# Norms in vector steps instead of a GpSimd power, a first triangle loaded in quarters, and a planner that looks ahead, in a delta-rule and two-MLP kernel

## The chip, the cores and the metric

The kernel runs on one core of one Trainium2 chip. The metric is device time in microseconds (us) of one execution. The profile is of one execution; its engines are PE (TensorE), DVE (VectorE), ACT (ScalarE), POOL (GpSimd) and SP (SyncE, which here only issues DMAs).

## The reference, cut to what matters

```python
# attention: batch 4, heads 8, 768 steps, head size 48
k_n = k / (np.linalg.norm(k, axis=-1, keepdims=True) + 1e-06)
for t in range(S):
    y[:, :, t] = np.einsum('bhd,bhde->bhe', q[:, :, t], state)
    v_old = np.einsum('bhde,bhd->bhe', state, kt)
    state = state + bt[:, :, :, None] * np.einsum('bhd,bhe->bhde', kt, vt - v_old)
# first MLP on 3072 tokens, 384 -> 1024 -> 384
h = x @ w_in
e = np.exp(h - np.max(h, axis=-1, keepdims=True))
solu = h * (e / (np.sum(e, axis=-1, keepdims=True) + 1e-09))
ln = (solu - mu) / np.sqrt(var + 1e-06) * g_ln        # mu, var over the 1024
x = ln @ w_out
# second MLP, 384 -> 2048 -> 384
h = x @ w_in2
g = h * (1.0 / (1.0 + np.exp(-1.702 * h)))
out = g @ w_out2
```

## The kernel before, in words

The 768 steps are cut into 24 chunks of 32 (`CH`). For a chunk, the recurrence inside it is a triangular system. `gram(n)` multiplies keys with keys and queries on PE, DVE masks the result (L659) and SP stores it to DRAM (`g_dr`, L681). Four chunks make one macro chunk (`m`, 0 to 5). `solve(m)` loads the four key products as one tile `tri` of 128 x 32 x 32 (L753; L706 in `solve0`), so that every partition holds one triangle. `roots` takes the diagonal, which holds the squared norms of the keys, raises it to the power 0.5 on POOL (L689) and makes from it, in five small DVE instructions (L694 to L698), the norm, its inverse square times beta, and the negative of that. The triangle is scaled and inverted by elimination on DVE (L768, L771; L722, L724 in `solve0`, which inverts two half triangles), scaled once more (`dsb`) and sent through DRAM to be laid out by chunk (`dt`). `recur(n)` (`first_recur` for the first four chunks) then carries the state through chunk n. `layer1(n)` is the first MLP up to its layer norm (tags A0 to A23), `layer1_out(g)` its second product for a group of four chunks (B0 to B5, L1122), `layer2(g)` the second MLP (C0 to C5, L1157 and L1184).

The weights come as 8-byte floats. `weights` loads a block into a stage buffer (L542), rebuilds single precision with ACT and DVE (L545, L549, L554, L562), and splits it into two half-precision parts (L575; L581, L582 on PE and L584 on ACT). This work stands beside the first four chunks. The setup also prepares two products for the first four chunks from the PSUM bank of the gram: `edges` on ACT (L670) and `place` on DVE (L674).

All five engines run their instructions in order, in an order that a planner writes at build time. Each piece of work is a task with an engine, a guessed duration, a priority and the keys that it reads and writes. The planner (`emit`) holds a clock for each engine; of the tasks of an engine that could start first it takes the one of lowest priority number. Priorities are a due time plus an offset from a table (`OFF`, one number for each tag and engine). Tasks of the first macro chunk have priorities below -20000 (up to -100000), and their tags get the letter F; before, the table held offsets of about the same size for those tags, which bring these priorities back to near zero, among those of the weights. Parameters stand in `PRM`. `busy` lets the planner fill an idle PE with products of zeros (L422).

Of the kernel before, what the change touches and what calls it, by code (L numbers as in the profile page):

```python
# [16 lines left out]
CH = 32  # L17
# [103 lines left out]
class Plan:  # L121
# [47 lines left out]
    def emit(self, sem=SEM, log=None):  # L169
        for t in self.tasks:  # L170
            t.left = len(t.deps)
            for d in t.deps:
                d.outs.append(t)
        for t in reversed(self.tasks):
            t.work2 = t.dur + (t.lat + LAND if t.lat else 0.0) + max([o.work2 + (sem if o.eng != t.eng or t.lat else 0.1) for o in t.outs], default=0.0)
        top = max(t.work2 for t in self.tasks)
        if PRM["al"]:
            for t in self.tasks:
                t.prio = (1 - PRM["al"]) * t.prio + PRM["al"] * PRM["af"] * (top - t.work2)
        free = {}  # L180
        pend = {}
        dma_free = 0.0
        bank_free = [0.0] * 8
        held = [False] * 8

        def place(b):
            open_ = [(bank_free[i], k, i) for k, i in enumerate(b.where) if not held[i]]
            return min(open_) if open_ else None

        for t in self.tasks:  # L190
            free.setdefault(t.eng, 0.0)
            pend.setdefault(t.eng, [])
            if t.left == 0:
                pend[t.eng].append(t)
        done = 0
        small, near = False, 0.0
        port = {"DVE": 0.0, "POOL": 0.0}
        clock = Clock()
        fetch = Fetch(clock)
        n = len(self.tasks)  # L200
        while done < n:
            cand = None
            for e, ts in pend.items():
                if not ts:
                    continue
                e0 = free[e]
                opts = []
                for t in ts:
                    st = max(e0, t.ready)
                    if t.lat:  # L210
                        st = max(st, dma_free - PRM["la"])
                    ok = True
                    for b in t.banks:
                        if b.at is None:
                            p = place(b)
                            if p is None:
                                ok = False
                                break
                            st = max(st, p[0])
                    if ok:  # L220
                        opts.append((st, t))
                if not opts:
                    continue
                first = min(o[0] for o in opts)
                opts = [o for o in opts if o[0] <= first + 1e-6]
                if e == "PE" and small:
                    opts = [o for o in opts if o[1].small and o[1].prio <= near] or opts
                st, t = min(opts, key=lambda o: (o[1].prio, o[1].idx))
                if cand is None or (st, t.prio, t.idx) < cand[0]:
                    cand = ((st, t.prio, t.idx), t)  # L230
            if cand is None:
                raise RuntimeError("no task can run")
            st, t = cand[0][0], cand[1]
            switch = t.eng == "PE" and t.small != small
            if t.eng == "PE":
                small, near = t.small, t.prio + PRM["near"]
            pend[t.eng].remove(t)
            for b in t.banks:
                if b.at is None:
                    b.at = place(b)[2]  # L240
                    held[b.at] = True
            dur = t.dur
            if t.eng == "PE":
                for gate, until, filler in self.fill:
                    if gate.end is None or held[0] or st > until:
                        continue
                    lo = max(free["PE"], gate.end + sem)
                    while True:
                        clock.run(lo, 0.0, 1.0)
                        if not (st - lo > (PRM["fg"] if clock.warm else 0.5) or clock.warm and clock.behind(lo) > 0.0):  # L250
                            break
                        filler()
                        free["PE"] = lo = fetch.run(lo, 0.216, 1.0, 2)
                st = max(st, free["PE"]) + (SWITCH[t.small] if switch else 0.0)
                dur = fetch.run(st, dur, t.work, t.count) - st
            elif t.port:
                other = port["POOL" if t.eng == "DVE" else "DVE"]
                dur = max(st + PORT[t.eng], other) + dur - PORT[t.eng] - st
                port[t.eng] = st + dur
            if log is not None:  # L260
                log.begin()
            t.fn()
            if log is not None:
                log.append((st, t))
            free[t.eng] = st + dur - TAIL.get(t.eng, 0.0)
            if t.lat:
                s2 = max(dma_free, st + dur)
                dma_free = s2 + t.lat
                t.end = s2 + t.lat + LAND
            else:  # L270
                t.end = st + dur + (DRAIN if t.eng == "PE" else 0.0)
            for b in t.banks:
                b.users -= 1
                if b.users == 0:
                    held[b.at] = False
                    bank_free[b.at] = t.end + sem
            for o in t.outs:
                o.left -= 1
                o.ready = max(o.ready, t.end + (sem if o.eng != t.eng or t.lat else OWN[t.eng] - (DRAIN if t.eng == "PE" else 0.0)))
                if o.left == 0:  # L280
                    pend[o.eng].append(o)
            done += 1
        return max(t.end for t in self.tasks)
# [3 lines left out]
def kernel(  # L287
# [160 lines left out]
    def dve(n, f=1.0):  # L448
        return 0.145 + f * n / 960.0
# [180 lines left out]
    def gram(n):  # L630
# [33 lines left out]
        if m == 0:  # L664
            v = bank_view = lambda: bank(bk).rearrange("p (h c) -> p h c", h=H)

            def edges():
                for b in range(B):
                    r, x = slice(32 * b, 32 * b + 16), 32 * (b % 2)
                    ACT.activation(out=EB[s][r, :, x + 16:x + 32], in_=v()[r, :, 16:32], func=ACTF.Copy)  # L670
            P.add("ACT", 1.2, edges, r=[bk], w=[f"E{s}"], prio=-3e4 + n)

            def place():
                DVE.tensor_tensor(  # L674
                    out=PB[s].rearrange("p h (x c) -> p h x c", x=2), in0=v()[:, :, CH:].unsqueeze(2).to_broadcast([128, H, 2, CH]),
                    in1=pm.unsqueeze(1).to_broadcast([128, H, 2, CH]), op=ALU.mult)
            P.add("DVE", dve(512), place, r=[bk, "pm"], w=[f"P{s}"], prio=-3e4 + n)
        else:
            P.add("DVE", dve(256), ev(p_, CH), r=[bk, "mask"], w=[gp[1]], prio=late)
# [7 lines left out]
    def roots(m, diag, prio):  # L687
        n_, c_, nn = nrm[:, 0], nrm[:, 1], nrm[:, 2]
        P.add("POOL", 0.8, lambda: POOL.tensor_tensor(  # L689
            out=nn, in0=diag, in1=half[:, 0:1].to_broadcast([128, CH]), op=ALU.pow),  # L690
            r=["tri", "half"], w=["nrm0", "nrm1"], prio=prio)

        def factors():
            DVE.tensor_scalar(out=n_, in0=nn, scalar1=1e-6, scalar2=None, op0=ALU.add)  # L694
            DVE.tensor_tensor(out=nn, in0=n_, in1=n_, op=ALU.mult)
            DVE.reciprocal(out=c_, in_=nn)
            DVE.tensor_tensor(out=c_, in0=c_, in1=btb[:, m], op=ALU.mult)
            DVE.tensor_scalar(out=nn, in0=c_, scalar1=-1.0, scalar2=None, op0=ALU.mult)  # L698
        P.add("DVE", 1.2, factors, r=["bt"], w=["nrm0", "nrm1"], prio=prio, port=True)

    def solve0():
        P.tag = "solve0"
        base = -9e4
        hc = CH // 2
        n_, c_, nn = nrm[:, 0], nrm[:, 1], nrm[:, 2]
        P.add("SP", ISSUE, lambda: SP.dma_start(out=tri, in_=g_dr[0]),  # L706
              r=[f"gdr0_{s}" for s in range(SUB)], w=["tri"], prio=base - 5, lat=dma(524288))
        roots(0, tri.rearrange("p i j -> p (i j)")[:, 0:CH * CH:CH + 1], base)
        cut = lambda x: x.rearrange("p (a i) -> p a i", a=2).unsqueeze(3).to_broadcast([128, 2, hc, hc])
        small = blocks[:, :, 0:hc, 0:hc]  # L710

        def scale():
# [555 lines left out]
```

## Time and profile before

| | |
|---|---|
| median of 3 runs | 848.41 us (845.32 to 852.46) |
| profiled execution | 848.33 us |
| its span, first to last instruction | 846.6 us |
| PE busy | 772.3 us (91%) |
| DVE busy | 550.9 us (65%) |
| ACT busy | 394.8 us (47%) |
| POOL busy | 285.9 us (34%) |
| mean granted TensorE clock | 0.968 |

The profiled execution took 848.33 us by the device's measure, 1.7 us more than its span. Busy shares are averages over a start of about 150 us, in which the first four chunks and the weights are worked on, and a long rest, in which PE works through the MLPs.

### The profile page before, as it was taken

Reading aid. Unit: us, or ns where it says so; the run is one execution under the profiler, and the core shown is the slowest. Engines: PE = TensorE matmul, PEld = TensorE weight load, DVE = VectorE, ACT = ScalarE, POOL = GpSimd, SP = SyncE. Lnnn points to the kernel's source line nnn. Section 1 sums busy time; section 2 is a strip of 40 time slices with the busy share of each in tenths; the row PEclk is TensorE's granted clock in tenths of the full one; section 3 lists DMA queues with packets and bytes.
Section 4 is the critical chain, followed back from the end, with each engine's and each line's share of the span. In section 5 each row is a group of like instructions: output and inputs, shape, how many; then the busy total and the mean of one; then the engine's idle time right before and its main releaser. Section 6 shows DMA issues by size and latency. Waiting matters only on the chain.

```text
span 846.6 us, 23757 instructions
## 1 busy us (share of the span) xinstructions
PE 772.3 (91%) x9981; PEld 390.7 (46%) x9981; DVE 550.9 (65%) x1324; ACT 394.8 (47%) x713; POOL 285.9 (34%) x259
## 2 busy tenths in 40 slices
PE   4399898979988999989998899999999999999997
PEld 3156664435544444444444344444444444444443
DVE  2677659968999898699965799765544283531111
ACT  4497548723655524435343444354445155452332
POOL 4230142032145713535331733522354024230322
PEclk9799899989999999989999999999999999999999
DMA  8788997844567836764457342544443342210000
GB/s 194 247 226 236 194 203 173 231 116 102 129 121 187 145 98 163 164 147 104 106 127 177 95 82 71 145 84 134 98 117 59 90 118 59 37 25 26 13 1 37
DMA packets 176922, 103.23 MB, mean 122 GB/s; under 512 B 127664, under 2 KB 163376, under 8 KB 176816
## 3 DMA queue, kind: packets, MB, share of 16 engines
q1 hardware_dynamic: 176816, 101.73, 51.0%
q8 instruction: 78, 1.28, 0.7%
q14 instruction: 28, 0.23, 0.1%
HBM read 64.26 MB, written 20.12 MB: 100 GB/s over the span
## 4 chain that ended last, share of the span: by engine, by line
PE 52%; DVE 30%; ACT 5%; DMA 4%; POOL 4%; issue 4%; SPq 1%; POOLq 0%; ACTq 0%; DVEq 0%
PE psum L1184 14%; PE psum L1157 13%; PE psum L1122 8%; PE psum L1050 7%; DVE trip L771 5%; DVE trt L768 4%; POOL nrm L689 3%; DVE mv L1011 3%; DVE thg L1165 2%; DVE eb L1069 2%; DVE mv L960 2%; DMA trip<-gdr 2%; PE psum L827 1%; PE psum L581 1%; DVE col L1057 1%
## 5 line engine op out<-in xcount | busy, mean ns | idle before, releaser
L1184 PE MATMUL psum<-thg,wo2h 128*128 128x512 f16 x576 | 192.3, 384 | 10.8 <-DVE thg L1174 5.0
L1171 POOL TENSOR_TENSOR thg<-thg 128x512 f16<-128x512 f32 x90 | 108.3, 1203 | 230.8 <-ACT thg L1168 152.4
L1157 PE MATMUL psum<-x2t,w2h 128*128 128x512 f16 x576 | 173.1, 382 | 2.0 <-DVE thg L1165 1.5
L1165 DVE SCALAR_TENSOR_TENSOR thg<-thg,psum 128x512 f32<-128x512 f32 x96 | 65.5, 683 | 87.6 <-ACT thg L1162 87.3
L1184 PE MATMUL psum<-thg,wo2l 128*128 128x512 f16 x288 | 110.6, 384 | 0.0
L1157 PE MATMUL psum<-x2t,w2l 128*128 128x512 f16 x288 | 110.1, 382 | 0.0
L1050 PE MATMUL psum<-w1h,xt 128*128 128x512 f16 x288 | 94.4, 391 | 5.0 <-DMA xt<-ysb 4.5
L1168 ACT ACTIVATE thg<-thg 128x512 f16<-128x512 f32 x96 | 60.2, 627 | 80.5 <-DVE thg L1165 78.8
L1162 ACT ACTIVATE thg<-psum 128x512 f32<-128x512 f32 x96 | 56.9, 593 | 81.1 <-PE psum L1157 80.5
L1184 PEld LDWEIGHTS <-wo2h 128*128 128x128 f16 x576 | 56.9, 99 | 77.6 <-issue 13.7
L1157 PEld LDWEIGHTS <-w2h 128*128 128x128 f16 x576 | 53.4, 98 | 64.7 <-issue 4.2
L771 DVE TENSOR_TENSOR trip<-trip,trt 128x30 f32<-128x30 f32 (+9 forms) x150 | 70.5, 470 | 2.8
L1066 ACT ACTIVATE eb<-psum,col 128x512 f32<-128x512 f32 x48 | 37.0, 773 | 75.2 <-DVE col L1062 70.6
L768 DVE TENSOR_TENSOR trt<-trip 128x30 f32<-128x30 f32 (+9 forms) x150 | 69.1, 460 | 2.5
L1050 PEld LDWEIGHTS <-xt 128*128 128x128 f16 x432 | 41.9, 100 | 58.1 <-issue 7.4
L1099 POOL TENSOR_TENSOR lnr<-eb,lnr 128x1024 f16<-128x1024 f32 x22 | 47.2, 2146 | 36.8 <-ACT lnr L1097 36.8
L1050 PE MATMUL psum<-w1l,xt 128*128 128x512 f16 x144 | 56.0, 389 | 0.0
L1122 PE MATMUL psum<-lnth,wo1h 128*128 128x512 f16 x144 | 54.6, 379 | 0.4 <-DVE eb L1069 0.4
L1122 PE MATMUL psum<-lnth,wo1l 128*128 128x512 f16 x144 | 54.6, 379 | 0.0
L1122 PE MATMUL psum<-lntl,wo1h 128*128 128x512 f16 x144 | 54.6, 379 | 0.0
L1057 DVE TENSOR_REDUCE col<-psum 128x1 f32<-128x512 f32 x48 | 32.9, 685 | 28.3 <-PE psum L1050 28.2
L1011 DVE SCALAR_TENSOR_TENSOR mv<-psum,mv 48x384 f32<-48x384 f32 x76 | 42.2, 555 | 12.4 <-PE psum L996 10.5
(208 smaller groups left out, 1178.3 us busy)
## 6 DMA issues: line engine op xcount, KB each, us to landing
kq<-kq SPq DMA_DIRECT2D x44, 192.0 KB, 4.6
stg<-w_in SPq DMA_DIRECT2D x13, 512.0 KB, 5.6
stg<-w_out SPq DMA_DIRECT2D x17, 384.0 KB, 4.2
vt<-vt SPq DMA_DIRECT2D x24, 192.0 KB, 3.3
kt<-kdr SPq DMA_DIRECT2D x48, 96.0 KB, 2.4
stg<-udr SPq DMA_DIRECT2D x48, 96.0 KB, 2.3
out<-ob SPq DMA_DIRECT2D x18, 256.0 KB, 2.1
st<-qt SPq DMA_DIRECT2D x40, 96.0 KB, 3.2
```

The source lines that it names most:

```text
L768: DVE.tensor_tensor(out=tv, in0=tri[:, lo:hi, j:j + 1].to_broadcast([128, nr, j]), in1=tri[:, j:j + 1, 0:j].to_broadcast([128, nr, j]), op ...
L771: DVE.tensor_tensor(out=tri[:, lo:hi, 0:j], in0=tri[:, lo:hi, 0:j], in1=tv, op=ALU.add)
L1011: P.add("DVE", dve(384), lambda sv=sv, r0=r0, e=e: DVE.scalar_tensor_tensor(out=sv, in0=bank(b4[e])[r0:r0 + D, 0:H * D], scalar=1.0 / (KS_ ...
L1050: PE.matmul(bank(bh[j]), lhsT=x[:, k], rhs=w_[:, k, 512 * j:512 * j + 512], start=(k == 0 and i == 0), stop=(k == K0 - 1 and i == 2))
L1099: P.add("POOL", pool(F1), lambda: POOL.tensor_tensor(out=ln_[1], in0=e_, in1=ln_[0], op=ALU.subtract), r=[lk[0]] + [f"eb{ie}_{j}" for j in ...
L1122: PE.matmul(bank(ba)[:, 0:w_], lhsT=wo1[a][:, k, oc], rhs=lnt[b][:, k, tk], start=(k == 0 and i == 0), stop=(k == K1 - 1 and i == 2))
L1157: PE.matmul(bank(bh)[:, 0:w_], lhsT=w2[a][:, k, fc], rhs=x2t[b][:, k, tk], start=(k == 0 and j == 0), stop=(k == K0 - 1 and j == 2))
L1162: P.add("ACT", act(w_), lambda: ACT.activation(out=th, in_=bank(bh)[:, 0:w_], func=ACTF.Tanh, scale=0.851 / (X2S * W2S)), r=[bh], w=[f"th{ ...
L1165: P.add("DVE", dve(w_), lambda: DVE.scalar_tensor_tensor(out=th, in0=th, scalar=1.0, in1=bank(bh)[:, 0:w_], op0=ALU.add, op1=ALU.mult), r= ...
L1168: P.add("ACT", act(w_), lambda: ACT.activation(out=gh, in_=th, func=ACTF.Copy), r=[f"th{i}"], w=[f"gh{i}"], prio=base)
L1171: P.add("POOL", pool(w_), lambda: POOL.tensor_tensor(out=gl, in0=th, in1=gh, op=ALU.subtract), r=[f"th{i}", f"gh{i}"], w=[f"gl{i}"], prio= ...
L1184: PE.matmul(bank(acc[o])[:, 0:w_], lhsT=wo2[a][:, f, oc], rhs=gb[i][b][:, 0:w_], start=(f == 0 and j == 0), stop=(f == K2 - 1 and j == 2))
```

## The change

Four edits. First, `roots` has no POOL instruction. DVE makes a first guess of a square root from the bits of the float (three instructions), then does three Newton steps of three instructions each (a reciprocal and two products), then the five instructions of `factors` as before. These are five tasks instead of a POOL task and a DVE task, in all six solves. Second, `solve0` loads its tile in four quarters of 32 partitions, each of which waits only for the store of its own chunk. Third, in the planner: on SP, DVE and ACT, a task of the first macro chunk (priority below -20000) that can start within 1.5, 0.3 or 0.3 us of the first possible start is taken ahead of everything else. `place` may not start before 15 us of the planner's clock. Fourth, the table of offsets: the 64 offsets of the F tags and of POOL in the solves are gone (so the first macro chunk keeps its priorities below -20000), and the other 485 all have new values. Three guessed durations in `solve0` are a little smaller.

```diff
+PRM = dict(kDVE=0.3, kACT=0.3, kPOOL=0.0, kPE=0.0, kSP=1.5, ...
                 first = min(o[0] for o in opts)
+                soon = [o for o in opts if o[1].prio < -2e4 and o[0] <= first + PRM["k" + e]] if PRM["k" + e] > 0 else []
+                if soon:
+                    st, t = min(soon, key=lambda o: (o[1].prio, o[1].idx))
+                    if cand is None or (st, t.prio, t.idx) < cand[0]:
+                        cand = ((st, t.prio, t.idx), t)
+                    continue
...
-            P.add("DVE", dve(512), place, r=[bk, "pm"], w=[f"P{s}"], prio=-3e4 + n)
+            P.add("DVE", dve(512), place, r=[bk, "pm"], w=[f"P{s}"], prio=-3e4 + n, nb=15.0)
...
     def roots(m, diag, prio):
         n_, c_, nn = nrm[:, 0], nrm[:, 1], nrm[:, 2]
-        P.add("POOL", 0.8, lambda: POOL.tensor_tensor(
-            out=nn, in0=diag, in1=half[:, 0:1].to_broadcast([128, CH]), op=ALU.pow),
-            r=["tri", "half"], w=["nrm0", "nrm1"], prio=prio)
+        u_, t_, s2 = nrm[:, 3], nrm[:, 2], nrm[:, 1]
+
+        def guess():
+            ui = u_.bitcast(I32)
+            DVE.tensor_scalar(out=s2, in0=diag, scalar1=2.0, scalar2=None, op0=ALU.mult)
+            DVE.tensor_scalar(out=ui, in0=diag.bitcast(I32), scalar1=1, scalar2=None, op0=ALU.logical_shift_right)
+            DVE.tensor_scalar(out=ui, in0=ui, scalar1=0x203D1DF5, scalar2=None, op0=ALU.add)
+
+        def heron():
+            DVE.reciprocal(out=t_, in_=u_)
+            DVE.tensor_tensor(out=t_, in0=s2, in1=t_, op=ALU.mult)
+            DVE.scalar_tensor_tensor(out=u_, in0=u_, scalar=0.5, in1=t_, op0=ALU.mult, op1=ALU.add)
 
         def factors():
-            DVE.tensor_scalar(out=n_, in0=nn, scalar1=1e-6, scalar2=None, op0=ALU.add)
+            DVE.tensor_scalar(out=n_, in0=u_, scalar1=0.5, scalar2=1e-6, op0=ALU.mult, op1=ALU.add)
...
-        P.add("DVE", 1.2, factors, r=["bt"], w=["nrm0", "nrm1"], prio=prio, port=True)
+        for f, d in ((guess, 0.55), (heron, 0.8), (heron, 0.8), (heron, 0.8), (factors, 1.2)):
+            P.add("DVE", d, f, r=["tri", "bt"], w=["nrm0", "nrm1"], prio=prio, port=True)
 
     def solve0():
...
-        P.add("SP", ISSUE, lambda: SP.dma_start(out=tri, in_=g_dr[0]),
-              r=[f"gdr0_{s}" for s in range(SUB)], w=["tri"], prio=base - 5, lat=dma(524288))
+        for s in range(SUB):
+            rows = slice(32 * s, 32 * s + 32)
+            P.add("SP", ISSUE, lambda rows=rows: SP.dma_start(out=tri[rows], in_=g_dr[0][rows]),
+                  r=[f"gdr0_{s}"], w=["tri"], prio=base - 5, lat=dma(131072))
...
-        P.add("DVE", 8.2, halves, w=["tri"], prio=base, port=True)
+        P.add("DVE", 7.8, halves, w=["tri"], prio=base, port=True)
...
-        P.add("DVE", 1.5, lambda: DVE.tensor_tensor(
+        P.add("DVE", 1.0, lambda: DVE.tensor_tensor(
```

## Rows read from the trace of the kernel before

**Rows 1.** The page, parts 1 and 4: busy times, and the chain by line

```profile
PE 772.3 (91%) x9981; PEld 390.7 (46%) x9981; DVE 550.9 (65%) x1324; ACT 394.8 (47%) x713; POOL 285.9 (34%) x259
PE psum L1184 14%; PE psum L1157 13%; PE psum L1122 8%; PE psum L1050 7%; DVE trip L771 5%; DVE trt L768 4%; POOL nrm L689 3%; DVE mv L1011 3%; DVE thg L1165 2%; DVE eb L1069 2%; DVE mv L960 2%; DMA trip<-gdr 2%; PE psum L827 1%; PE psum L581 1%; DVE col L1057 1%
```

**Rows 2.** Windows by stage: busy time of each engine, granted clock, DMA share, GB/s

```profile
0.00:41.00 41.00, 15.63 (x330) 9.64 (x331) 18.49 (x56) 17.44 (x39) 15.10 (x39) 0.88 0.86 227
...
71.00:154.00 83.00, 75.90 (x1529) 47.72 (x1528) 59.38 (x167) 52.13 (x101) 19.69 (x12) 0.92 0.93 200
...
180.00:540.00 360.00, 329.51 (x4610) 163.76 (x4609) 302.68 (x719) 158.42 (x280) 149.30 (x120) 0.97 0.55 124
540.00:846.00 306.00, 298.13 (x2822) 140.93 (x2820) 122.32 (x284) 126.63 (x215) 93.38 (x82) 1.00 0.28 67
```

**Rows 3.** The chain that ended last, in order of time, 15 to 31 us

```profile
15.54 4.23 DMA gdr<-gsb
19.84 4.83 DMA trip<-gdr
24.74 5.77 POOL nrm L689
```

**Rows 4.** Timeline of DVE at the start and after the first power

```profile
14.49 0.69 DVE L674 TENSOR_TENSOR ktr<-psum,lnr 128x512 f32<-128x512 f32 x1 [1.17 <-ACT st L670]
15.10 0.41 DVE L659 TENSOR_TENSOR gsb<-psum,mask 128x256 f32<-128x256 f32 x1
...
30.53 0.18 DVE L694 TENSOR_SCALAR nrm<-nrm 128x32 f32<-128x32 f32 x1 [3.96 <-POOL nrm L689]
30.75 0.19 DVE L695 TENSOR_TENSOR nrm<-nrm 128x32 f32<-128x32 f32 x1
30.97 0.35 DVE L696 RECIPROCAL nrm<-nrm 128x32 f32<-128x32 f32 x1
31.36 0.19 DVE L697 TENSOR_TENSOR nrm<-nrm,bt 128x32 f32<-128x32 f32 x1
```

**Rows 5.** Timeline of PE: the last of the first four grams

```profile
12.61 1.12 PE L648 MATMUL psum<-kq 48*32 48x64 f32 x33 [0.44 <-issue]
```

**Rows 6.** DMA issues: KB of one, median us from issue to landing

```profile
st<-pdr SPq DMA_DIRECT2D x80, 32.0 KB, 2.1
```

**Rows 7.** Waits: who waited for whom, us in total, times, longest

```profile
DVE nrm L694 <- POOL nrm L689: 20.4, 5, 6.0
```

**Rows 8.** Timeline of PE behind three of the later powers

```profile
186.42 1.01 PE L1184 MATMUL psum<-thg,wo2h 128*128 128x512 f16 x2 [4.97 <-DVE thg L1174]
...
194.03 0.60 PE L1157 MATMUL psum<-x2t,w2h 128*128 128x512 f16 x2
...
366.11 0.37 PE L941 MATMUL psum<-mv,ktr 48*32 48x48 f32 x4 [3.58 <-DVE mv L1011]
...
479.05 0.38 PE L1184 MATMUL psum<-thg,wo2h 128*128 128x512 f16 x1 [2.19 <-ACT thg L1168]
```

**Rows 9.** Timeline of DVE at three of the later powers

```profile
186.28 0.68 DVE L1165 SCALAR_TENSOR_TENSOR thg<-thg,psum 128x512 f32<-128x512 f32 x1
...
358.14 0.88 DVE L694 TENSOR_SCALAR nrm<-nrm 128x32 f32<-128x32 f32 x1 [4.60 <-POOL nrm L689]
...
483.39 0.67 DVE L1165 SCALAR_TENSOR_TENSOR thg<-thg,psum 128x512 f32<-128x512 f32 x1
483.99 0.20 DVE L768 TENSOR_TENSOR trt<-trip 128x58 f32<-128x58 f32 x1
```

**Rows 10.** Timeline of SP, ACT and PE: first weight load, w1's last part and first use, B0

```profile
11.57 0.58 SPq L542 DMA_DIRECT2D stg<-w_in  x1
...
54.72 0.60 ACT L584 ACTIVATE w1l<-psum 128x512 f16<-128x512 f32 x1
...
70.98 0.39 PE L1050 MATMUL psum<-w1h,xt 128*128 128x512 f16 x1
...
154.32 0.38 PE L1122 MATMUL psum<-lnth,wo1h 128*128 128x512 f16 x1
```

More of the change, by code (lines that the diff above doesn't have):

```diff
@@ new lines @@
+PRM = dict(kDVE=0.3, kACT=0.3, kPOOL=0.0, kPE=0.0, kSP=1.5, s0=0, s1=3, wb=21.5, bl=161.965, vm=-0.684, vo=-1.262, pe=38.322, near=22.976, al=0.0, af=0.658, xp=25.764, lp=1.945, go1=24.87, so1=49.904, ew=48, nx=6.743, kp=13.711, need=100.793, fg=0.161, f1=0.0, f3=1796.849, sp=0.084, gp=0.667, gq=99, cold=25.151, cf=-1.14, nb4=9.499, v1b=1.424, cut=0.473, el=22.0, la=0.602, d0=-55.31, d1=-18.518, d2=6.18, d3=1.2, a0=14.438, wo1s=1.606, nk=15.164, nb2=1.269, nb3=7.307, early=21.447, v1=-9.577, wa=0.829, U=36.161, T0=31.882, g0=0.697, a=-0.318, b=0.937, ao=18.661, go=231.282, gs=-2.989, so=-0.04, ss=0.661, w1=-840.745, wo1=-7.28, w2o=-52.255, w2s=8.446, wo2o=41.493, wo2s=4.056, nb=1.319, bs=0.333, cs=4.152, su=8.832, ld=47.69)
```

3 lines of the change are left out of this document (1 added, 2 removed).

## The prediction

> **What bounds the kernel now.** I began with the page. PE is busy 91% of the span, and the chain by line is mostly PE, but POOL's L689, the power, holds 3% of it, with six instructions in the whole run [rows 1]. Then the windows by stage [rows 2], where PE's idle time is the length less its busy time. From 180 to 540 us it is 360.0 - 329.5 = 30.5 us, with the clock at 0.97; in the first 41 us it is 25.4 us; from 71 to 154 us 7.1 us. The last 306 us have next to none before the end, and nothing in the change can help there. From 180 us on every idle microsecond of PE is paid in full, because PE's work is fixed. Before that the path is the first four chunks: gram, triangle, recurrence, first MLP, until the second product (B0) starts at 154.32 us [rows 10].
>
> The chain in time shows the start of that path: a store of the key products, 4.23 us to landing; the load of the triangle, 4.83 us; the power, 5.77 us [rows 3]. DVE does nothing useful in the end of that time, and its next instruction, L694, starts at 30.53 us [rows 4].
>
> In the later solves DVE runs in order, and L694 stands in its queue until POOL is done: five such waits, 20.4 us together, the longest 6.0 us [rows 7]. What matters is what is queued behind. At 178 to 186 us it is L1165, which feeds L1184, and PE stands still for 4.97 us; at 362 us it is the state update L1011, and PE stands 3.58 us; at 476 us again L1165, by way of ACT, and PE stands 2.19 us [rows 8, 9]. After such a stop two matmuls take 1.01 us instead of 0.60 [rows 8], so PE works for a while at the lower of its two levels (1.2 instead of 2.4 GHz); at 194.03 us the pace is back. The power's planned duration is 0.8 us and its real one over 5 us, so the planner had no reason to put other work in between.
>
> **The change part by part.**
>
> *The first triangle.* The last of the four masks runs at 15.10 us, behind `place` of the chunk before, which itself waited for ACT [rows 4]. The last gram ends at 12.61 + 1.12 = 13.73 us [rows 5]. With `place` held back the mask can start at about 13.8 us: 1.3 us saved. The store then takes 4.23 us, or less where the look-ahead keeps weight loads out of SP's queue in between; down to 2.1 us, what the smallest transfers take [rows 6]. I take 3.5 us, nearer the row of the same store, so 0.7 us saved. The last quarter load takes between 2.1 us [rows 6] and the 4.83 us of the whole [rows 3]; I take 3.0 us, since it is a quarter of the bytes and the three others are on their way: 1.8 us saved.
>
> The Trainium skill (DMA: Bandwidth & Descriptors, Rules for kernel authors) speaks against the quarters: two transfers to disjoint halves of the partitions share the same engines, so one transfer of all partitions should be used. By it the 1.8 us would be nothing, and the forecast 1.8 us longer. No run here shows it; it speaks of transfers that could all start together, which these cannot.
>
> *The power, first solve.* From its start to the first instruction behind it, 30.53 - 24.74 = 5.8 us go [rows 3, 4]. In its place come three one-source instructions at 0.22 us from start to start and three Newton steps of a reciprocal (0.39) and two more (0.23 each): 0.66 + 3 x 0.85 = 3.2 us [rows 4]. Saved: 2.6 us. The first solve is then 1.3 + 0.7 + 1.8 + 2.6 = 6.4 us earlier; by the bounds of the two transfers between 3.9 and 8.7 us. I pass this on whole to B0, as PE then has no other work that counts.
>
> *The order of the start.* The first macro chunk now goes ahead of the weights everywhere. Where the recurrence stood behind weight work on DVE and ACT this gains; but DMA is 93% busy from 71 to 154 us [rows 2], and the weights must still come. I take nothing, with bounds of 10 us gained (more than the 7.1 us of idle time, for some of PE's work there is filler) and 6 us lost.
>
> *The later powers.* What the three stops cost: the idle times of 4.97, 3.58 and 2.19 us, 10.7 us, and, for the lower clock, an estimated 2 us each (4 us at half the pace, out of the at most 7.6 us between 186.42 and 194.03 us [rows 8]), 6 us: 17 us in all. If the Newton steps stand in one piece in DVE's queue, 3.2 us a solve, 16 us for the five later ones, take the place of 20.4 - 4.0 = 16.4 us of waits [rows 4, 7]: next to nothing is won on DVE, and only the three long stops shrink, by 2.8 us (6.0 - 3.2), 1.4 us (4.60 - 3.2 [rows 7, 9]) and about 1 us, 5 us together. But they are five tasks of at most 1.2 us, and the planner puts other work between tasks of a solve: L1165 stands amid the elimination at 483.39 us [rows 9]. Then nothing behind waits longer than about a microsecond, and nearly all 17 us come back. I take 12 us, between 5 and 17.
>
> *What it costs.* Each later solve puts 3.2 us more work on DVE, which is 302.7 of 360.0 us busy from 180 to 540 us [rows 2]; the removed waits make room for it. Two things can make it dearer. The short instructions after the power were slow at times: L694 took 0.88 us at 358.14 us instead of 0.18 [rows 4, 9], while POOL worked off what had queued behind its power. With the power gone that queue is not there, but POOL does run beside the new steps. And now DVE, not POOL, waits for the triangle to land, with L1165 and the state updates queued behind it. I take 3 us for both, with bounds of 0 and 10 us.
>
> The Trainium skill (GPSIMD Engine Reference, Specifications) has the first of these: POOL shares its way to memory with DVE, and contends with DVE instructions of two inputs, as two of the three in a Newton step are. The slow rows agree; by the rule alone the new steps would always be slow beside POOL.
>
> *The offsets.* All 485 that remain are new, so the order of PE's work from 180 to 540 us changes as well. The trace can't price this: of the 30.5 us of idle time there some 20 us are not the power's, and another order can have 10 us more or less of that. I take nothing, since no row favours a side.
>
> *The sum*, against the profiled execution: 848.3 - 6.4 - 12 + 3 = 833 us. Its time is that of the median (848.41 us), so this is also the forecast for the median.
>
> **The rivals.** (1) The start gives nothing: the first triangle comes earlier, but DMA and the weights set B0's time all the same. For it speaks the DMA share of 0.93; against it that PE has idle time and filler before B0. It gives 848.3 - 9 = 839 us. (2) The Newton steps stand in one piece, or wait for the triangle: the later solves give 5 us, the cost of 3 us stays, and the time is 848.3 - 6.4 - 2 = 840 us. (3) The order of the start gains its 10 us, and the later stops vanish: 848.3 - 16 - 14 = 818 us. (4) Slower: the weights come too late. SP holds their first load, at 11.57 us before [rows 10], until the last quarter is issued, by the sum above about 17 to 18 us, 6 us later, and the priorities put DVE's and ACT's weight work behind the recurrence for a second delay. The first MLP needs w1, whose last part was ready at 55.3 us and first used at 70.98 us [rows 10]: 15.7 us of slack, of which 6.4 us go to the earlier chain and 6 us to the later load. When the second delay is more than the 3 us that remain, the first MLP stands still on PE, whose queue is in order, and the recurrence behind it. If w1 is worked on only in the gaps of all four chunks it can be 25 to 30 us late; with the 9 us of the later solves that is 848.3 + 27 - 9 = 866 us. The planner knows the weights' durations, which speaks against so much. (5) The new offsets cost what the rest gains, 10 us and more: 845 to 850 us.
>
> **How the numbers follow.** Forecast (826 to 838 us) 0.45; rival 1 0.12, rival 2 0.13, rival 3 0.12, rival 4 0.08, rival 5 0.10. The range reaches from rival 3 to the upper end of rival 5: 817 to 850 us; outside it are rival 4 and a little of both ends. About 1% is what a measurement of this kernel can tell from no change, so faster means under 840 us: the forecast, rival 3, most of rival 1 and half of rival 2, 0.74. Within 1%: the rest of those and rival 5, 0.17. Slower: rival 4 and the end of rival 5, 0.09.
>
> **What would show it.** In the changed kernel L689 is gone from POOL, the last quarter lands at about 20 to 21 us instead of 24.7, the elimination of the first solve starts some 6 us earlier, and B0 starts before 150 us. From 180 to 540 us (shifted) PE idles some 20 instead of 30 us, with no stop of 3 us behind a solve, and other DVE work stands between the Newton steps. I am wrong if DVE waits long for the triangle's load, if the small steps take 0.8 us and more, if PE waits for w1 or w2 parts, or if new stops of PE appear at places that have nothing to do with the solves.

## The result, and the profile after

The changed kernel takes 820.12 us (median of 4 runs, 818.51 to 821.19) beside 850.43 us for the kernel before (845.32 to 854.63; one run more than the three ahead of the prediction). The ratio is 0.964, with a 95% interval of 0.958 to 0.970. The profiled execution took 821.19 us, of which the span is 819.5 us; against the 848.33 us of the profiled execution before it is 27.1 us shorter. The forecast was 833 us, in a range of 817 to 850 us.

The page, part 1, of the new kernel, and under it the windows by stage with the same edges as before. After the length stand the busy times of PE, PEld, DVE, ACT and POOL with their instructions, then the granted clock, the DMA share and GB/s:

```profile
PE 757.7 (92%) x9965; PEld 383.0 (47%) x9965; DVE 562.0 (69%) x1396; ACT 392.4 (48%) x713; POOL 255.0 (31%) x253
```

```profile
0.00:41.00 41.00, 16.72 (x271) 9.45 (x272) 22.52 (x69) 19.18 (x41) 9.36 (x38) 0.68 0.81 216
71.00:154.00 83.00, 76.48 (x1342) 44.59 (x1338) 61.70 (x182) 55.55 (x106) 11.92 (x9) 0.98 0.84 198
180.00:540.00 360.00, 340.36 (x4838) 170.28 (x4837) 315.48 (x796) 160.67 (x285) 133.37 (x118) 0.99 0.58 136
```

From 180 to 540 us PE now idles 360.0 - 340.4 = 19.6 us, where it was 30.5 us [rows 2]. The stretch from 71 to 154 us hardly differs in PE's idle time, but there is other work in it: the second product, B0, starts in it. The clock of 0.68 in the first 41 us is of this execution: it is 1.00 there in the profiles of five of the kernels below that keep its order. The timeline of SP, ACT and PE, in the places that answer to [rows 10]:

```profile
12.49 1.63 SPq L548 DMA_DIRECT2D stg<-w_in  x1
...
47.62 0.58 ACT L590 ACTIVATE w1l<-psum 128x512 f16<-128x512 f32 x1
...
65.60 0.39 PE L1068 MATMUL psum<-w1h,xt 128*128 128x512 f16 x1
...
133.14 0.38 PE L1140 MATMUL psum<-lnth,wo1h 128*128 128x512 f16 x1
```

B0 comes at 133.14 us instead of 154.32, 21.2 us sooner. That is not all gain, as PE has not done the same work by then. The windows split at B0, first of before, then of the new kernel; each time all of PE, its grams alone (L648, now L654) and its matmuls of zeros alone (L422, now L428):

```profile
0.00:154.32 154.32, 118.96 (x2381) 73.96 (x2382) 102.92 (x265) 96.49 (x194) 42.29 (x57) 0.91 0.90 211
154.32:846.60 692.28, 653.31 (x7602) 316.77 (x7599) 448.03 (x1060) 298.30 (x520) 243.62 (x202) 0.98 0.43 102
0.00:154.32 154.32, 20.97 (x960) 17.76 (x960) 0.91 0.90 211
0.00:154.32 154.32, 12.59 (x43) 4.24 (x43) 0.91 0.90 211
```

```profile
0.00:133.14 133.14, 99.83 (x1966) 61.93 (x1967) 88.60 (x229) 91.20 (x184) 30.56 (x55) 0.88 0.81 202
133.14:819.50 686.36, 657.88 (x8000) 321.07 (x7998) 473.44 (x1167) 301.23 (x529) 224.44 (x198) 0.99 0.47 111
0.00:133.14 133.14, 12.95 (x576) 11.29 (x576) 0.88 0.81 202
0.00:133.14 133.14, 5.22 (x15) 1.67 (x15) 0.88 0.81 202
```

Of the 1536 matmuls of the 24 grams, 960 ran ahead of B0 and now 576 do: 8.0 us of PE's work only moved behind B0. Without the grams PE reaches B0 13.2 us sooner (7.4 us fewer zeros, which like idle time stand where PE has nothing of its own to do, 2.1 us less idle time, 3.7 us less for the other matmuls), and behind B0 it needs 11.4 us less, with 28.5 us of idle time instead of 39.0; the grams themselves take 2.5 us less. Over the whole run the 27.1 us are 12.5 us less idle time, 3.8 us fewer zeros and 10.8 us less for the same 9938 other matmuls. The last goes with the granted clock, 0.98 instead of 0.92 from 71 to 154 us and 0.99 instead of 0.97 from 180 to 540 us; no run changes the clock alone. The weights are not late: w1's last part is ready at 47.6 us and used from 65.6 us on.

The first triangle, in the timeline of DVE and of SP (what [rows 3, 4] showed of before):

```profile
12.13 0.42 DVE L665 TENSOR_TENSOR psb<-psum,mask 128x256 f32<-128x256 f32 x1 [0.69 <-PE psum L654]
...
23.20 0.69 DVE L568 SCALAR_TENSOR_TENSOR fst<-stg,fst 128x512 int32<-128x512 int32 x1
23.81 0.18 DVE L699 TENSOR_SCALAR nrm<-trip 128x32 f32<-128x32 f32 x1
...
26.62 0.19 DVE L706 SCALAR_TENSOR_TENSOR nrm<-nrm 128x32 f32<-128x32 f32 x1
26.84 0.18 DVE L709 TENSOR_SCALAR nrm<-nrm 128x32 f32<-128x32 f32 x1
```

```profile
14.22 0.39 SPq L687 DMA_DIRECT2D gdr<-psb  x1
...
18.89 0.31 SPq L724 DMA_DIRECT2D trip<-gdr  x1
```

The last mask runs 3.0 us sooner than before. Its store is issued only at 14.22 us, behind the weight load that holds SP for 1.63 us from 12.49 us on, and the last quarter of the load at 18.89 us; it took 4.1 us to landing. The guess (L699) starts at 23.81 us, 0.8 us after that, right behind a piece of weight work (L568) in DVE's own queue. From its start to the factors (L709) go 3.0 us, where the power took 5.8 us. The factors come at 26.84 instead of 30.53 us: 3.7 us, not 6.4.

The later solves, in the waits of DVE and in its timeline at the fourth solve:

```profile
DVE nrm L699 <- DMA trip<-gdr: 7.1, 3, 4.1
```

```profile
370.39 0.81 DVE L705 TENSOR_TENSOR nrm<-nrm 128x32 f32<-128x32 f32 x1
371.23 0.77 DVE L706 SCALAR_TENSOR_TENSOR nrm<-nrm 128x32 f32<-128x32 f32 x1
371.92 0.54 DVE L1050 TENSOR_REDUCE col<-psum 128x1 f32<-128x384 f32 x1
...
374.51 0.68 DVE L1183 SCALAR_TENSOR_TENSOR thg<-thg,psum 128x512 f32<-128x512 f32 x1
375.11 0.35 DVE L704 RECIPROCAL nrm<-nrm 128x32 f32<-128x32 f32 x1
...
375.94 1.18 DVE L709 TENSOR_SCALAR nrm<-nrm 128x32 f32<-128x32 f32 x1
```

The 20.4 us in which DVE waited for POOL [rows 7], 4.0 of them in the first solve, are gone; in their place it waits 7.1 us for a triangle to land. Between the Newton steps stands other work, L1183 among it, the line that PE had waited for [rows 9]. PE's longest stop after B0 is this one, and no solve is behind it; the longest before was 4.97 us [rows 8]:

```profile
217.12 0.92 PE L1019 MATMUL psum<-mv,kt 32*48 32x48 f32 x32 [2.04 <-DVE eb L1087]
```

### The profile page after: what moved, and what is told of

Read it like the earlier page. It is cut to its first block, busy times and chain, and to the rows that moved or that the text cites. A ratio compares the mean times of both kernels' runs of the same rounds, so it can differ in the third digit from the quotient of the medians.

```text
span 819.5 us, 23840 instructions
## 1 busy us (share of the span) xinstructions
PE 757.7 (92%) x9965; PEld 383.0 (47%) x9965; DVE 562.0 (69%) x1396; ACT 392.4 (48%) x713; POOL 255.0 (31%) x253
## 5 line engine op out<-in xcount | busy, mean ns | idle before, releaser
L1183 DVE SCALAR_TENSOR_TENSOR thg<-thg,psum 128x512 f32<-128x512 f32 x96 | 65.4, 682 | 87.8 <-ACT thg L1180 87.6
L786 DVE TENSOR_TENSOR trt<-trip 128x30 f32<-128x30 f32 (+9 forms) x150 | 65.7, 438 | 3.1
L789 DVE TENSOR_TENSOR trip<-trip,trt 128x30 f32<-128x30 f32 (+9 forms) x150 | 63.7, 424 | 3.1
L1068 PE MATMUL psum<-w1l,xt 128*128 128x512 f16 x144 | 55.1, 383 | 0.0
L1105 POOL TENSOR_TENSOR col<-col,half 128x1 f32<-128x1 f32 x24 | 13.7, 570 | 122.8 <-DVE col L1103 98.1
```

Of the source, the lines that this page charges most:

```text
L786: DVE.tensor_tensor(out=tv, in0=tri[:, lo:hi, j:j + 1].to_broadcast([128, nr, j]), in1=tri[:, j:j + 1, 0:j].to_broadcast([128, nr, j]), op ...
L789: DVE.tensor_tensor(out=tri[:, lo:hi, 0:j], in0=tri[:, lo:hi, 0:j], in1=tv, op=ALU.add)
L1068: PE.matmul(bank(bh[j]), lhsT=x[:, k], rhs=w_[:, k, 512 * j:512 * j + 512], start=(k == 0 and i == 0), stop=(k == K0 - 1 and i == 2))
L1183: P.add("DVE", dve(w_), lambda: DVE.scalar_tensor_tensor(out=th, in0=th, scalar=1.0, in1=bank(bh)[:, 0:w_], op0=ALU.add, op1=ALU.mult), r= ...
```

## The experiments

The question after the result was why B0 comes 21 us sooner, as the first triangle has only 3.7 of them. Theory A: from the order of the start, which works off the first macro chunk ahead of the weights. Theory B: from the norms. Theory C: from the new table of offsets. Theory D: from the look-ahead and not the priority. The twelve runs below were timed beside the kernel before, which had medians of 848.7, 848.0 and 849.2 us in the three sessions; ratios are to it.

**The power back in the new order.**

```diff
-            DVE.tensor_scalar(out=s2, in0=diag, scalar1=2.0, scalar2=None, op0=ALU.mult)
-            DVE.tensor_scalar(out=ui, in0=diag.bitcast(I32), scalar1=1, scalar2=None, op0=ALU.logical_shift_right)
-            DVE.tensor_scalar(out=ui, in0=ui, scalar1=0x203D1DF5, scalar2=None, op0=ALU.add)
+            POOL.tensor_tensor(out=nn, in0=diag, in1=half[:, 0:1].to_broadcast([128, CH]), op=ALU.pow)
...
-            DVE.reciprocal(out=t_, in_=u_)
-            DVE.tensor_tensor(out=t_, in0=s2, in1=t_, op=ALU.mult)
-            DVE.scalar_tensor_tensor(out=u_, in0=u_, scalar=0.5, in1=t_, op0=ALU.mult, op1=ALU.add)
...
```

> The new kernel in its own order, with the single GpSimd power put back in place of the guess and the three Newton steps; the same norms are computed to rounding. Theory A (the gain comes from the first macro chunk being worked off ahead of the weights; the power is worth its 2.6 us in the first solve and part of the later stops): 820 + 2.6 + about 10 = 830 to 836 us, and the second product B0 starts within 4 us of 133 us. Theory B (the norms are most of the gain): 842 us or more, and B0 is late by more than 8 us.

Measured: 829.13 us (825.44 to 831.14), ratio 0.978 (0.974 to 0.982), B0 at 132.70 us. Near A's 830 to 836 us, and far from B's 842. The norms have 829.1 - 820.1 = 9.0 us (11 by the ratios); the other 20 us (848.7 - 829.1) are there with the power too. B0 is no later here, and its PE has the same 576 gram matmuls and 15 of zeros ahead of B0. Behind B0 PE idles 36.3 us, where the new kernel has 28.5. Where the time goes is seen in its waits of DVE, its DVE at one power, and the longest PE stop, which comes after it:

```profile
DVE nrm L705 <- POOL nrm L699: 22.9, 5, 7.6
```

```profile
290.29 0.81 DVE L705 TENSOR_SCALAR nrm<-nrm 128x32 f32<-128x32 f32 x1 [7.62 <-POOL nrm L699]
...
296.56 0.88 PE L963 MATMUL psum<-rb,dt 32*32 32x48 f32 x64 [3.41 <-DVE rb L958]
```

**The Newton steps in the old order**, in one piece where the power stood, every other instruction as before:

```diff
-        P.add("POOL", 0.8, lambda: POOL.tensor_tensor(
-            out=nn, in0=diag, in1=half[:, 0:1].to_broadcast([128, CH]), op=ALU.pow),
-            r=["tri", "half"], w=["nrm0", "nrm1"], prio=prio)
...
+        P.add("POOL", 0.8, newton, r=["tri", "half"], w=["nrm0", "nrm1"], prio=prio)
...
```

> The kernel before in its own order, with the guess and the three Newton steps on VectorE standing in one piece where the power stood. Theory A: 2.6 us from the first solve and about 5 us from the later three stops, 840 to 846 us, with B0 still later than 148 us. Theory B (norms are most of the gain): 828 to 834 us. A third case (DVE's Newton steps wait for the triangle with other work behind them and nothing is won): 848 to 852 us.

Measured: 843.50 us (839.65 to 846.52, 10 runs), ratio 0.993 (0.990 to 0.996), so 3 to 8 us gained, and B0 at 156.15 us. As A had it; B is out. The gain is all behind B0, where PE idles 33.4 us instead of 39.0. Its windows and PE's timeline show that the stop of 4.97 us [rows 8] has shrunk, not gone, since 3 us of steps stand in DVE's queue instead of a wait:

```profile
180.00:540.00 360.00, 335.48 (x4639) 166.44 (x4638) 316.69 (x772) 161.58 (x285) 132.36 (x118) 0.97 0.57 129
```

```profile
185.85 0.38 PE L1193 MATMUL psum<-thg,wo2h 128*128 128x512 f16 x1 [2.05 <-ACT thg L1177]
```

**The priority alone, with the old table:** the kernel before, without the offsets that took the first macro chunk's tasks down.

```diff
-'Fgram0|SP': 99772.64
-'Fgram0|PE': 100025.97
...
-'FA3|POOL': 37150.4
```

> The kernel before, with the offsets of the first macro chunk alone taken out of the table, so that its tasks keep the priorities they are added with and go ahead of the weights; the power stays, the triangle comes in one load, and there is no look-ahead. Theory A (this priority is the main gain): 850 - 14 = 832 to 840 us, and B0 starts at 136 to 144 us instead of 154. Theory B (norms): 846 to 852 us and B0 within 4 us of 154. A theory D (it is the look-ahead and not the priority, since without it an engine takes what can start first whatever its priority): also 846 to 852 us, told from B by the run without look-ahead.

Measured: 891.65 us (886.40 to 894.21), ratio 1.051 (1.046 to 1.056): 43 us slower, which neither theory had. B0 starts at 151.53 us, but the factors of the second solve come at 170.41 us instead of 126.47, and PE fills its gaps with matmuls of zeros, 43 of them and 12.6 us before, and here, by the page's part 5, 141 and 36.3 us:

```profile
L422 PE MATMUL psum<-zeros 128*128 128x512 f16 x141 | 36.3, 400 | 14.4 <-DVE zeros L421 14.4
```

So an earlier B0 is no gain by itself. That the table's other offsets fit only the order they were made for is the likely reason; no run here shows it.

**The old values of the remaining offsets, in the new kernel:**

```diff
-'w1_0_0|PE': 894.42
+'w1_0_0|PE': 1145.86
...
```

> The new kernel with the 485 remaining offsets at their old values. Theory A says that the gain is made before B0 (133 us) and kept: 818 to 828 us, B0 within 3 us of 133. Theory C (the new offsets are a large part of the gain, because the old ones were made for the old order): 835 us or more, with more PE idle time after 180 us than the 20 us of the new kernel.

Measured: 860.73 us (854.23 to 864.75), ratio 1.015 (1.008 to 1.022), B0 at 167.41 us. Slower than the new kernel by 41 us, and than the one before by 12: A's number was wrong, C's right, but not its place: from 180 to 540 us PE idles 22.5 us, hardly more than the 19.6 of the new kernel. The place is seen in ACT and in PE, around w1's last part:

```profile
54.55 0.58 ACT L590 ACTIVATE w1l<-psum 128x512 f16<-128x512 f32 x1
...
121.79 0.60 ACT L590 ACTIVATE w1l<-psum 128x512 f16<-128x512 f32 x1 [3.63 <-PE psum L588]
```

```profile
119.26 2.07 PE L587 MATMUL psum<-fst,eye 128*128 128x512 f32 x2
121.12 0.63 PE L588 MATMUL psum<-w1h,neg 128*128 128x512 f16 x1
121.55 1.91 PE L428 MATMUL psum<-zeros 128*128 128x512 f16 x4
123.25 0.63 PE L1068 MATMUL psum<-w1h,xt 128*128 128x512 f16 x1
```

Five of w1's six low parts are ready by 55.1 us, the sixth at 122.4, because PE makes the product for it only at 119.26 us, and the first MLP's matmuls with it start at 123.25 us at once. All six high parts were ready by 44.3 us, so no load was late: PE's order was. In the old table the offset of one of these six products, 1145.86, stands well above the other five (735 to 972); that it is the one which waits fits, but no run changes it alone.

**Four kernels with a plain table.** Both tables were made for one order each, so the offsets were set to nothing in both kernels, but for the tasks without a tag, and in the first kernel for the first macro chunk's. The steps from one to the next are then the priority; the norms, the quarters and the later `place`; and the look-ahead.

```diff
-'w1_0_0|SP': 875.96
-'w1_0_0|ACT': 688.89
...
+'w1_0_0|SP': 0.0
+'w1_0_0|ACT': 0.0
...
```

> The kernel before with every offset of the table set to nothing, but for those of the first macro chunk (which take its tasks down to the priorities of the others) and of the tasks without a tag. First of four kernels that share this plain table, so that no table favours one order of the start. By itself: slower than the kernel before, 870 to 900 us; the second product B0 is later than 154 us.

> As the kernel before with the plain table, and the offsets of the first macro chunk gone too: its tasks go ahead of the weights wherever both can start. Theory A (the priority gains by itself; the 891 us with the old table was that table's fault): 10 us or more faster than the plain table with the first macro chunk among the others. Theory C (there is no gain in the priority; the gain lies in the table that was made for it): within 8 us of it, or slower.

> The new kernel with the plain table and the look-ahead set to nothing on all engines: first macro chunk on top, Newton steps and quarter loads, but an engine takes what can start first. Theory A: 8 to 14 us faster than the same without Newton steps and quarters, by the 5 to 9 us that the power was worth in both orders and some 3 us of the first triangle.

> The new kernel with the plain table, look-ahead in. If the look-ahead is what lets the first macro chunk through (theory D): 8 us or more faster than without it, B0 earlier by as much. Theory A without D: within 5 us of it. Theory C: the four kernels with the plain table differ by no more than the 12 us that norms and triangle are worth, and none of them comes near 820 us.

Measured, in this order: 900.76 us (900.02 to 901.44), 872.77 (867.93 to 874.33), 852.05 (850.22 to 856.01) and 849.34 (847.41 to 850.60); B0 at 243.46, 153.76, 158.80 and 156.51 us. The second is 28 us faster than the first, as A had it. But the first is not the order of the kernel before with the table away: w1's own priority is about -840, and only its offsets, 487 to 1146, bring it among the first macro chunk's. Without them w1 goes ahead: its first high part is ready at 8.7 us instead of 20.2, and the factors of the first solve come at 40.36 us instead of 30.53. The 28 us are the first macro chunk ahead of w1 against behind it; what it is worth against among it, as before, no run shows. They are also not B0's 90 us: the first kernel has 18 of its 24 grams done at B0, the second 12. The norms with the quarters and `place` are worth 21 us here, more than the 8 to 14 expected; the look-ahead 3 us with ranges that touch, so D is out, with this table at least. C's "no more than 12 us" is out too, but it is right in that none comes near 820 us: a table is worth 901 - 848 = 53 us in the old kernel and 849 - 820 = 29 us in the new one. The stretch from 180 to 540 us, of the second and the third:

```profile
180.00:540.00 360.00, 328.90 (x4555) 162.72 (x4557) 313.03 (x730) 167.53 (x304) 144.31 (x114) 0.98 0.56 139
```

```profile
180.00:540.00 360.00, 341.58 (x4753) 170.67 (x4752) 321.66 (x782) 174.72 (x314) 133.64 (x118) 1.00 0.59 140
```

PE idles 31.1 us there with the power and 18.4 without it, 12.7 us less, where it is 6.0 us less in the old order with its table and 5.1 us in the new one. A table that steers round the power's waits would explain the difference; no run shows it.

**The first triangle, term by term.** Four kernels with the new kernel's order of instructions and one edit each. One load in place of four:

```diff
-            P.add("SP", ISSUE, lambda rows=rows: SP.dma_start(out=tri[rows], in_=g_dr[0][rows]),
+            P.add("SP", ISSUE, (lambda: SP.dma_start(out=tri, in_=g_dr[0])) if s == SUB - 1 else (lambda: None),
```

> The new kernel, every instruction in its order, but the first triangle in one load at the place of the last quarter. The prediction's term (the last quarter is 1.8 us sooner than the whole): the guess starts 1.8 us later than 23.8 us, the whole run takes 821 to 823 us. Rival by the rule of the Trainium skill (DMA: Bandwidth & Descriptors, Rules for kernel authors: one transfer of all partitions rather than disjoint halves), as the weight load in SP's queue sets the time of the last quarter anyway: the guess starts within 0.7 us of 23.8 us, 819 to 821 us. For both a part of the delay may be given back before B0.

`place` not held back (only DVE's order changes, at the four places before the last mask):

```diff
-            P.add("DVE", dve(512), place, r=[bk, "pm"], w=[f"P{s}"], prio=-3e4 + n, nb=15.0)
+            P.add("DVE", dve(512), place, r=[bk, "pm"], w=[f"P{s}"], prio=-3e4 + n)
```

> The new kernel without the holding back of place; the order of all engines but DVE is the same, and DVE's differs only in the four places before the masks' end. The prediction's term (the last mask runs 1.3 us sooner with place held back): the last mask is at 13.5 us or later instead of 12.1, the guess up to 1.5 us later, 820 to 822 us. Rival: SP issues the store of the last mask only at 14.2 us, behind a weight load, so the mask has 2 us of room and the guess moves by less than 0.5 us: no change, 819 to 821 us.

The fourth mask's store ahead of the weight load in SP's queue, written at the place where the tasks are issued:

```diff
-            t.fn()
+            stores += t.eng == 'SP' and t.tag.startswith('Fgram') and t.dur == ISSUE; late.append(t.fn) if t.eng == 'SP' and t.tag.startswith('w1') and stores == 3 else t.fn(); late[:] = [f() for f in late][:0] if stores == 4 else late
```

> The new kernel with one swap in SP's queue: the store of the fourth mask is issued ahead of the weight load that it stands behind. If that weight load is why the first triangle gained 3.7 us instead of 6.4: the store is issued by 12.8 us instead of 14.2, the last quarter by 17.5 instead of 18.9, the guess starts by 22.6 us instead of 23.8, and 818 to 820 us. If the landing of the last quarter is set by the traffic of the loads beside it: the guess starts within 0.5 us of 23.8 us, 819 to 821 us.

The same with two Newton steps:

```diff
-            DVE.reciprocal(out=t_, in_=u_)
+            steps.append(0); len(steps) % 3 and DVE.reciprocal(out=t_, in_=u_)
...
```

> As the swap in SP's queue, and with two Newton steps instead of three (the norms then agree to about 5e-7 instead of 1e-7). If each step costs its 0.85 us on VectorE and the path holds it in the first solve and in part of the later ones: 0.9 us more in the first solve and 1 to 2 us in the later five, 815 to 818 us. If the later ones are hidden in gaps of VectorE: 817 to 819 us. A version that should beat both kernels.

Measured, in this order: 818.12 us (817.41 to 823.53), 823.42 (818.98 to 827.77), 823.03 (818.26 to 830.53) and 820.35 (817.77 to 823.90), with ratios of 0.965 (0.961 to 0.968), 0.969 (0.966 to 0.973), 0.970 (0.966 to 0.975) and 0.966 (0.962 to 0.970). None is told apart from the new kernel's 0.964 (0.958 to 0.970), and none beats it: the hoped-for version with two steps doesn't either. The traces tell more. DVE of the kernel with one load, where the load took 5.6 us from issue to landing; then of the one with place free, of the one with the store first, and of the one with two steps as well:

```profile
22.05 0.69 DVE L568 SCALAR_TENSOR_TENSOR fst<-stg,fst 128x512 int32<-128x512 int32 x1
23.29 0.19 DVE L699 TENSOR_SCALAR nrm<-trip 128x32 f32<-128x32 f32 x1 [0.55 <-DMA trip<-gdr]
```

```profile
15.16 0.41 DVE L665 TENSOR_TENSOR psb<-psum,mask 128x256 f32<-128x256 f32 x1
...
25.53 0.18 DVE L699 TENSOR_SCALAR nrm<-trip 128x32 f32<-128x32 f32 x1
```

```profile
24.84 0.69 DVE L568 SCALAR_TENSOR_TENSOR fst<-stg,fst 128x512 int32<-128x512 int32 x1
25.45 0.18 DVE L699 TENSOR_SCALAR nrm<-trip 128x32 f32<-128x32 f32 x1
```

```profile
24.96 0.18 DVE L699 TENSOR_SCALAR nrm<-trip 128x32 f32<-128x32 f32 x1
...
27.17 0.18 DVE L709 TENSOR_SCALAR nrm<-nrm 128x32 f32<-128x32 f32 x1
```

With one load the guess starts no later than with four, at 23.29 us, so no gain of the quarters shows; the rival had it. With the store first the guess starts later, at 25.45 us, against both expectations. That profile doesn't test the swap cleanly: its last mask ran at 14.03 us, so the store came at 14.48, no sooner than 14.22. The kernel with two steps as well does: mask at 13.20, store at 13.66, last quarter issued at 16.57 us, 2.3 us sooner, and the guess still at 24.96. The weight load moved behind the store (14.07 and 14.89 us instead of 12.49) is the one whose conversion ACT waits for, and this feeds L568, which stands ahead of the guess on DVE; also the last quarter takes 6.7 us to landing there instead of 4.1. So the swap delays what the guess stands behind. With place free the last mask is at 15.16 us instead of 12.13 and the guess at 25.53, again right behind L568; its first part was as expected, and the 3 us of the median are within the spread of the runs. The third step is 0.85 us on the path of the first solve, as expected (2.2 us from guess to factors instead of 3.0); its worth in the whole run can't be told from nothing.

## Why the prediction held, and which step of it failed

The forecast was 13 us too long by the median (12 by the profiled execution), inside its range. By the two profiled executions 13.2 of the 27.1 us were won ahead of B0, 11.4 behind it and 2.5 in the grams, which moved across it; the forecast had 6.4 us ahead of B0 and 9 behind it.

*What bounds the kernel.* This held. PE idles 19.6 us from 180 to 540 us, where "some 20" was said; no stop of 3 us stands behind a solve; L689's waits are gone; and B0 starts before 150 us. One reading was off: of the five waits of [rows 7] four are in the later solves and one, 3.96 us, in the first; the sum took that one out again.

*The order of the start: taken at 0, with 10 us for its gain at most. This is the step that failed.* Ahead of B0 PE has 7.4 us fewer zeros and 2.1 us less idle time, and its other matmuls take 3.7 us less: 13.2 us, of which the first triangle can have 3.7 at most. So the order, with the table that goes with it, has 9.5 us or more by these two profiles, next to the bound that the prediction had named for just this filler and idle time. The zeros belong to the order; the rest is less sure, as in the five other profiles of this order PE idles 32.8 to 35.2 us ahead of B0 (33.3 here, 35.4 before). The run with the power back has the same zeros and grams ahead of B0, and B0 no later, so no part of the norms in it shows. The reason for the zero, that DMA was 93% busy, did not show: that share fell to 0.84 in the same stretch, at as many GB/s (198, 200 before).

*The offsets: taken at 0, give or take 10 us, as a term of its own.* No run gives such a term. With the old offsets the new order loses 12 us against the kernel before; the priority with the old table, without the look-ahead and the rest, loses 43 us. Order and table are worth about 20 us together (848.7 - 829.1 us, with the power kept) and these runs don't price them one by one. The slower rival, the weights too late for the first MLP, was priced at 866 us, and the new order with the old table, where w1's last part comes at 122.4 us, takes 861 us. That the two are close is luck: the rival had the loads and the work of DVE and ACT late, and there it was PE's order. In the new kernel the first weight load is issued at 12.49 us, 0.9 us later than before and not 6.

*The first triangle: 6.4 us, measured 3.7.* Its power term was right (2.6 us; 5.8 - 3.0 = 2.8 us measured). The other three, 3.8 us, gave 0.9 us (24.74 to 23.81 us). The mask gained 3.0 us in this profile (1.0 us at the least in the other three named at the end), but the store stands behind a weight load on SP and takes 4.7 us instead of the 3.5 taken, the last quarter takes 4.1 us instead of 3.0, and DVE's own queue holds the guess for 0.8 us more. The bound of 2.1 us for both transfers came from a row over the whole run. That the triangle's gain reaches B0 whole, as the prediction took it, no run shows: with the Newton steps in the old order the factors come 1.4 us sooner and B0 1.8 us later.

*The later powers: 12 us less 3.* This held. Behind B0 11.4 us were gained between the two profiles, 10.5 of them idle time. The run with the power back puts the norms at 9.0 us in all by the medians, and its B0 is no later, so they are put to the later ones. Both costs that it set against the gain are there, the 7.1 us of waits for the triangle and small instructions of 0.77 to 1.18 us beside POOL; no stop of PE over 2.04 us came of them. The rival that the steps stand in one piece gave 848.3 - 2.6 - 2 = 843.7 us when its other triangle terms are left out; the run that does just this took 843.5 us. The sum came out, but its 2.6 us for the first solve do not show at B0: that run's gain is all behind it.

The rival that came nearest, with 818 us, had the order of the start gain its 10 us and the stops vanish, 16 us ahead of B0 and 14 behind it; measured are 13.2 and 11.4 us, and 2.5 in the grams.

## What to carry to other kernels

An order and a table of offsets that was made for it are one change: with the table of the other order either kernel lost. A table set to nothing is no neutral ground either, as here its offsets also held w1 back. The time of one landmark is a gain only if the same work lies ahead of it: count what moved across. Before an instruction is to start earlier, look at its own engine's queue too: here the weight work in front of the guess held it 0.8 us after its data had landed, and a swap on SP that issued the load sooner delayed that work. A long instruction on another engine is paid by what is queued behind the wait; short tasks in its place are worth more where other work may stand between them.

## What was not expected of the hardware

A quarter of the triangle (128 KB) took 4.1 to 6.0 us from issue to landing in the new kernel, and the whole (512 KB) 5.6 us in the kernel with one load and 4.83 us before [rows 3]: its size hardly mattered at the start, where the DMA engines are 81 to 86% busy. The Trainium skill (DMA: Bandwidth & Descriptors, Rules for kernel authors) advises one transfer of all partitions instead of two to disjoint halves; the runs here agree in that the parts show no gain, 818.1 us with one load and 820.1 us with four.

Small DVE instructions were stretched to the length of a POOL instruction beside them. This one of POOL runs beside L709 above, which took 1.18 us there and 0.18 us in the first solve, though it reads one tensor only:

```profile
375.93 1.16 POOL L1189 TENSOR_TENSOR thg<-thg 128x512 f16<-128x512 f32 x1
```

The Trainium skill (GPSIMD Engine Reference, Specifications) names DVE instructions with two inputs, and those in a mode that uses two ports, as the ones that contend; the row fits, if L709 runs in such a mode, which no run here shows. The slow row that the prediction cites, L694, has one input too; those of two inputs beside it in the same solve, L695 and L697, took 1.09 and 1.66 us.

The start varies from one execution to the next: with the same order of instructions on PE, DVE, ACT and POOL, the last mask ran at 12.13, 13.20, 14.03 and 14.05 us in four profiles. A term of 1 or 2 us in the first 20 us can't be read from a single one. B0 varies more: 133.14, 134.78, 137.53 and 143.09 us in the same four, the last in the slowest execution profiled of them (830.53 us), with a granted clock of 0.90 from 71 to 154 us instead of 0.96 to 1.00.
